# Scores in four quarters, zeros split around the attention, and weight pieces in fewer, larger transfers

## The chip, the cores and the metric

The kernel runs on one core of a Trainium2 chip. A core has a matrix engine (TensorE, "PE" in the profile, with its weight loads listed apart as "PEld"), a vector engine (DVE), a scalar engine (ACT), a general one (POOL), and a sync engine (SP) whose queue issues most DMAs. Sixteen DMA engines move the data between HBM and the on-chip memories. The metric is the device time of one execution in microseconds, the median of several runs.

## The reference

Two blocks follow each other. The first is attention in chunks: 4 batches x 8 heads, 768 positions of 64 numbers. Each chunk of 32 queries sees 8 memory keys, 16 positions to its left, itself, and 8 to its right. The second is a mixture of 8 experts over the 3072 resulting rows of 512 numbers: each row goes to the expert with the largest logit, each expert keeps at most 80 rows, and all other rows of the output are zero.

```python
scores = scale * np.matmul(q_c, k_full.transpose(0, 1, 3, 2))
a = np.exp(scores - max); a = a / sum(a)
out[:, :, c_start:c_end] = np.matmul(a, v_full)
...
x = attn_out.transpose(0, 2, 1, 3).reshape(B * S, H * D)
out = np.zeros((N, D))
for e in range(E):
    tok_idx = rows of expert e, the `capacity` with the largest gate weight
    h = np.maximum(x[tok_idx] @ w1[e], 0.0)
    out[tok_idx] = gate_w[tok_idx, None] * (h @ w2[e])
```

## The kernel before

**Attention** runs over 32 units (`units`, L770): a unit is one pair of heads and one half of the positions, so 384 queries per head. A unit's scores (`scores`, L773) are held transposed, keys on the 128 partitions and queries along the row: four groups of 96 queries, each with its own window of 128 keys (8 memory keys and 120 positions). First one bf16 matmul per head puts the mask into the whole score tile `sp` (L779), then four fp32 matmuls per head add keys times queries (L786). The two heads lie on partitions 0 to 63 and 64 to 127, so the two heads' matmuls use the two row halves of the array. The profile lists each fp32 matmul as two instructions. ACT then takes the exponential (L794), and the next iteration multiplies by the values (L357), in four column tiles of 32, and divides by the sum (L364, L366). Other work of a unit: transposes that put k and q into shape (L343, L315), transposes of the result for the gates (L375), and one step of the ranking that finds each expert's 80 best rows.

The order on each engine is written out by hand: `in_order` fixes the order in which the loop at L852 names the instructions. On the sync queue each iteration names, in this order, a load of k or q four units ahead (L889), the values six units ahead (L894), every fourth unit a store of finished rows into `xd` in HBM (L896), and then some bulk transfers (L897 to L905). Bulk means weights (`slow`) and zeros for the output (`nothing`).

**Weights.** Each expert has two matrices of 2 MB. Matrices are counted through, so matrix 2e is w1 of expert e and 2e+1 is w2 (`Weights`, L169). Nine have a place at once (WR = 9). Matrices 0, 1, 3 and 4 are loaded during the attention; matrix 2 lies where the k and q loads land (`ld`), so it is added to `slow` at unit NU - 6 = 26 (L897). Matrices 5 to 8 lie in memory that the attention gives up, and are loaded after it (L1143); 9 to 15 follow when an expert has freed a place (`load_next`, L1024). Each matrix is loaded in eight pieces of 256 KB: 128 rows of 512 numbers.

**Pacing.** From the end of the attention on, pieces go through `paced` (L162): each new piece waits until the one six before it has landed.

**Zeros** are 24 pieces of 128 output rows (L192), written from the tile `zero`. All of them fit into the loop.

**Experts** run in `run_experts` (L997), after an interlude in which the last ranks are found and the rows are gathered. For each expert: `up` (L1029, matmuls at L1043) with w1, `turn_in`, `store` of the one before, `down` (L1050, matmuls at L1057) with w2, and at the end `last` (L1065, matmuls at L1077). The scatter of an expert's rows into the output (L1111, L1099) comes after the zeros.

Of the kernel before, what the change touches and what calls it, by code (L numbers as in the profile page):

```python
# [12 lines left out]
F32 = mybir.dt.float32  # L13
# [11 lines left out]
NG = 4  # L25
# [37 lines left out]
def kernel(  # L63
# [13 lines left out]
    nc = tc.nc  # L77
    B, H, S, D = q.shape
    N, DM = out.shape
    E = moe_w_gate.shape[1]  # L80
    F = moe_w1.shape[2]
# [6 lines left out]
    NU = NR * HP  # L88
    DK = DM // 128
    FK = F // 128  # L90
# [3 lines left out]
    WR, WR0, WR2 = 9, 2, 2  # L94
# [9 lines left out]
    const = ctx.enter_context(tc.tile_pool(name="const", bufs=1))  # L104
# [24 lines left out]
    oneb = const.tile([128, 1], BF16, name="oneb")  # L129
    pref = const.tile([128, E], F32, name="pref")  # L130
    over_s = const.tile([128, NU, 2, NT], F32, name="over_s")
    zero = const.tile([128, DM], F32, name="zero")
    xg0 = const.tile([cap, DM], F32, name="xg0")
    xn0 = const.tile([128, HP, cap], F32, name="xn0")
    zerob = zero[:, :64].bitcast(BF16)
# [14 lines left out]
    follow = mybir.DependencyInfo(mybir.DependencyClass.Sync, mybir.DependencyReason.DATA)  # L150
# [8 lines left out]

    pieces = deque()  # L160

    def paced(dma):  # L162

        dma()
        pieces.append(list(nc.cur_bb.bb.instructions)[-1])
        if len(pieces) > 6:
            tc.add_manual_dep(pieces[-1], pieces.popleft().name, follow, reason="pieces")

    class Weights:  # L169
        def __init__(self, pools, tag):  # L170
# [2 lines left out]
        def load(self, i):  # L173
            src, nch = ((moe_w1, DK), (moe_w2, FK))[i % 2]
            s = i % len(self.pools)
            if i in self.given:
                t = self.given[i].rearrange("p a b -> p (a b)").rearrange("p (a b) -> p a b", a=nch)
            else:
                t = self.pools[s].tile(
                    [128, nch, DK * F // nch], F32, name=f"w{i}", tag=f"{self.tag}{s}", bufs=1  # L180
                )
            self.t[i] = t

            return [
                lambda c=c, f=f: nc.sync.dma_start(
                    t[:, c, f : f + 512], src[i // 2, c * 128 : c * 128 + 128, f : f + 512]
                )
                for c in range(nch)
                for f in range(0, DK * F // nch, 512)
            ]  # L190

    def zeros():  # L192
        zrows = 128
        return [
            lambda i=i: nc.sync.dma_start(
                out[i * zrows : (i + 1) * zrows, :].rearrange("(p r) d -> p r d", p=128),
                zero.unsqueeze(1),
            )
            for i in range(N // zrows)
        ]  # L200

# [506 lines left out]
    W = Weights([wpool] * (WR0 + 1 + WR2) + [None] * (WR - WR0 - 1 - WR2), "w")  # L708
    W.given[WR0] = wpool.tile([128, 4, F], F32, name="ld", tag=f"w{WR0}", bufs=1)

    with ExitStack() as actx:
# [61 lines left out]
        def scores(i):  # L773
            n, f = units[i]
            sp = [ps_s.tile([WK, NG, GQ], F32, name="sp", tag="s") for e in range(2)]

            for e in range(2):
                r = slice(64 * e, 64 * e + 64)
                nc.tensor.matmul(  # L779
                    sp[e].rearrange("p g q -> p (g q)"), lhsT=mkey[r, f, :], rhs=mqry[r, f, :],  # L780
                    start=True, stop=False,
                )
            for g in range(NG):
                for e in range(2):
                    r = slice(64 * e, 64 * e + 64)
                    nc.tensor.matmul(  # L786
                        sp[e][:, g], lhsT=at.kT[n][r, NG * f + g, :],
                        rhs=at.qT[n][r, HT * f + GQ * g : HT * f + GQ * g + GQ], start=False,
                        stop=g == NG - 1,
                    )  # L790
            P[i] = []
            for e in range(2):
                P[i].append(wk.tile([WK, NG, GQ], F32, name="P", tag="P"))
                nc.scalar.activation(P[i][e], sp[e], Act.Exp, scale=scale)  # L794
# [24 lines left out]
            turns[i] = turns.get(i, []) + [("k", n)]  # L819
            turns[i + 1] = turns.get(i + 1, []) + [("q", n)]  # L820

        later, done = deque(), deque()
        ranks = Ranks(gt, ps_x)
        start = len(list(nc.cur_bb.bb.instructions))
        def fill_in(n, cols=128):
# [26 lines left out]
        for i in range(NU):  # L852
            n, f = units[i]
            r = i // HP
            if i + 1 < NU:
                scores(i + 1)
            for kind, m in turns.get(i, []):
                if kind == "k":
                    at.turn_k(m)
                elif i >= 2:  # L860
                    at.turn_q(m)
            if i in constants:
                constants[i]()
            if i + 2 < NU:
                at.put_mv(*units[i + 2])
            if later:
                later.popleft()()
            if i:
                turn_x(i - 1)
            if i < 2:  # L870
                at.turn_q(i + 2)
            values(i)
            if i and i % HP == 0:
                lus[r] = ps_x.tile([128, 512], F32, name="lu", tag="t")
                steps = ranks.steps(r - 1, [xTs[i - HP + c] for c in range(HP)], lus[r])
                later = deque(
                    [lambda last=last, first=first: (last(), first()) for last, first in zip(later, steps)]
                    + steps[len(later) :]
                )
            if later:  # L880
                later.popleft()()
            if i == NU - 2:
                lp = at.pt[0]

                nc.tensor.matmul(lp[:, : NT * E], lhsT=zerob, rhs=zerob[:, : NT * E], start=True, stop=False)
                early([0, 1], lp)
            if i == NU - 1:
                early([2], lp)
            for kind, m in turns.get(i, []):  # L889
                (at.load_k if kind == "k" else at.load_q)(m + 2)  # L890
            if i % (2 * HP) == 1 and i + 7 < NU:
                at.load_mv(i // (2 * HP) + 1)
            if i + 6 < NU:
                at.load_v(*units[i + 6])  # L894
            if i and i % HP == 0:
                at.store(r - 1, xr[r - 1])  # L896
            if i == NU - 6:  # L897
                slow += W.load(WR0)
            for _ in range(2 if i >= 4 else 0):
                bulk = slow if slow and (i >= NU - 6 or i % 4 < 3) else nothing  # L900
                if bulk:
                    bulk.popleft()()
            for _ in range(2 if i >= 20 and i % 2 == 0 else 0):
                if nothing:
                    nothing.popleft()()  # L905
        turn_x(NU - 1)
        at.store(NR - 1, xr[NR - 1])
        assert not slow
        for dma in nothing:
            paced(dma)  # L910


        r = NR - 1
# [234 lines left out]
    with tc.If(redo[1] > 0):  # L1148

        with ExitStack() as actx:  # L1150
# [7 lines left out]
            at.load_mem(nc.sync)  # L1158
            at.clear()
            at.turn_mem(ps_t.tile([128, 512], F32, name="pm2", tag="t"))  # L1160
            for dma in zeros():
                dma()
            ranks = Ranks(gt, ps_t)
            for i, (n, f) in enumerate((HP * b + c, f) for b in range(B) for f in range(2) for c in range(HP)):
# [60 lines left out]
        with ExitStack() as fctx:  # L1225
            fw2 = fctx.enter_context(tc.tile_pool(name="fw2", bufs=1, reuse_waits="tile"))
            W2 = Weights([fw2] * 2, "v")
            for i in range(2):
                for dma in W2.load(i):
                    dma()  # L1230
            run_experts(fctx, "2", W2)

# [27 lines left out]
```

## Time and profile before

| what | value |
|---|---|
| median of 3 runs | 247.33 us (247.24 to 256.02) |
| span of the profiled execution | 246.5 us |
| TensorE busy | 228.3 us, 93% |
| weight loads busy | 200.6 us, 81% |
| DVE, ACT, POOL busy | 43%, 33%, 33% |
| moved by DMA | 70.97 MB, mean 288 GB/s |
| weight pieces | 128 of 256 KB, 5.2 us to land (the 8 of matrix 2: 6.0) |
| zeros | 24 pieces of 256 KB, 4.9 us to land |

The page's slices cut the span into 40 parts of 6.2 us; a digit is the busy share in tenths, and the last row is what the DMA engines moved.

```profile
PE   5979999999999999999899999969799997999980
PEld 3857889798888788888778889959799996999970
...
DMA  6999999999999999999999899999999998890101
GB/s 205 284 283 298 279 296 325 340 370 321 341 364 330 376 331 334 370 278 329 302 305 372 264 363 307 295 333 298 311 335 313 358 288 284 277 332 28 32 29 37
```

The attention fills the slices up to about the 22nd, the interlude the next two, the experts the rest. TensorE is nearly full in most slices, and so are the DMA engines until slice 36. A matmul's end is modelled, so a busy TensorE need not be one at its peak. Two of the groups that the change touches:

```profile
L786 PEld LDWEIGHTS sp<-qT,kT 64*128 64x128 f32 x512 | 33.2, 189 | 1.5 <-issue 0.9
L786 PE MATMUL sp<-qT,kT 64*128 64x96 f32 x512 | 33.5, 269 | 0.9 <-ACT qT L316 0.4
```

Here "64*128" says that 64 rows and 128 columns of the array hold weights; "64x96" is what streams through them.

### The profile page before, as it was taken

The numbers are of one execution on the slowest core, as the hardware profiler recorded it, in microseconds if no ns is written. First come the engines' busy times: TensorE is split into PE (matmuls) and PEld (weight loads), VectorE is DVE, ScalarE is ACT, GpSimd is POOL, SyncE is SP. The second block draws the span as 40 slices with busy tenths as digits, with TensorE's granted clock in tenths as the row PEclk, the third lists the DMA queues.
The fourth block names the chain that finished last, engine by engine and source line by source line (L and its number), as shares of the span: only waits on it lengthen the run. The fifth ranks groups of instructions, "written<-read, shape, count | busy, mean of one in ns | idle before, by whom it ended". The sixth has DMA issues, their size and how long they took to land. (4 is left out here: it accounts for less than half of the span.)

```text
span 246.5 us, 11417 instructions
## 1 busy us (share of the span) xinstructions
PE 228.3 (93%) x4976; PEld 200.6 (81%) x4976; DVE 105.5 (43%) x288; ACT 81.8 (33%) x198; POOL 80.5 (33%) x182
## 2 busy tenths in 40 slices
PE   5979999999999999999899999969799997999980
PEld 3857889798888788888778889959799996999970
DVE  3333447758579477585555862000112111110240
ACT  2245555665555573665545301100000101010000
POOL 2454947537275182450412147300101010110111
PEclk9999999999999999999999889989999999999996
DMA  6999999999999999999999899999999998890101
GB/s 205 284 283 298 279 296 325 340 370 321 341 364 330 376 331 334 370 278 329 302 305 372 264 363 307 295 333 298 311 335 313 358 288 284 277 332 28 32 29 37
DMA packets 69879, 70.97 MB, mean 288 GB/s; under 512 B 38204, under 2 KB 46396, under 8 KB 69820
## 3 DMA queue, kind: packets, MB, share of 16 engines
q1 hardware_dynamic: 67836, 67.17, 87.4%
q0 software_dynamic: 1024, 2.62, 3.5%
q8 instruction: 41, 0.67, 1.2%
q10 hardware_dynamic: 960, 0.36, 0.6%
q14 instruction: 18, 0.15, 0.2%
HBM read 56.24 MB, written 13.89 MB: 285 GB/s over the span
## 5 line engine op out<-in xcount | busy, mean ns | idle before, releaser
L794 ACT ACTIVATE P<-sp 128x384 f32<-128x384 f32 x64 | 27.9, 488 | 29.6 <-PE sp L786 29.6
L1043 PE MATMUL hp<-xn,w 128*64 128x80 f32 x896 | 33.7, 233 | 3.0 <-issue 3.0
L1043 PEld LDWEIGHTS hp<-xn,w 128*64 128x64 f32 x896 | 32.1, 137 | 3.9 <-issue 3.4
L786 PEld LDWEIGHTS sp<-qT,kT 64*128 64x128 f32 x512 | 33.2, 189 | 1.5 <-issue 0.9
L786 PE MATMUL sp<-qT,kT 64*128 64x96 f32 x512 | 33.5, 269 | 0.9 <-ACT qT L316 0.4
L1057 PE MATMUL yt<-hT,w 128*64 128x80 f32 x896 | 34.2, 239 | 0.0
L1057 PEld LDWEIGHTS yt<-hT,w 128*64 128x64 f32 x896 | 33.0, 142 | 1.2 <-issue 1.1
L1047 ACT ACTIVATE hT<-hp 128x320 f32<-128x320 f32 x16 | 7.0, 437 | 70.7 <-PE hp L1043 70.7
L1111 POOL DMA_INDIRECT out_dram<-y,idx_s x7 | 6.4, 917 | 73.0 <-DVE y L1110 73.0
L357 PE MATMUL o<-vw,P 128*32 128x65 f32 x1536 | 28.9, 222 | 0.7 <-issue 0.7
L357 PEld LDWEIGHTS o<-vw,P 128*32 128x32 f32 x1536 | 23.5, 109 | 6.3 <-issue 5.4
L346 DVE COPY kT<-pt 128x480 f32<-128x480 f32 x32 | 19.9, 666 | 16.3 <-PE pt L343 8.2
L268 POOL COPY vw<-mv 8x512 f32<-8x512 f32 x32 | 22.4, 703 | 8.7 <-DMA vw<-in_v_dram 8.7
L1022 DVE COPY xn<-xp 128x320 f32<-128x320 f32 x7 | 3.4, 491 | 39.4 <-PE xp L1020 39.4
L366 DVE TENSOR_TENSOR xr<-o,over_s 128x384 f32<-128x384 f32 x32 | 17.8, 558 | 1.1
L316 ACT COPY qT<-pt 128x384 f32<-128x384 f32 x31 | 16.0, 582 | 4.8 <-PE pt L315 4.8
L377 ACT COPY xT<-xt 128x384 f32<-128x384 f32 x32 | 15.7, 489 | 4.7 <-PE xt L375 4.7
L330 POOL COPY kh<-ld 128x768 f32<-128x768 f32 x15 | 12.3, 822 | 13.7 <-PE more L549 8.3
L375 PE MATMUL xt<-ident,xr 128*128 128x128 f32 x96 | 16.5, 281 | 0.0
L315 PE MATMUL pt<-ident,qh 128*128 128x128 f32 x96 | 15.0, 291 | 1.2 <-DVE kT L346 1.2
L1063 DVE COPY ys<-yt 128x320 f32<-128x320 f32 x7 | 3.4, 492 | 28.7 <-PE yt L1057 28.7
L531 DVE SCALAR_TENSOR_TENSOR less<-gbs,gw,behind 128x384 bf16<-128x384 f32 x21 | 15.0, 745 | 0.0
(162 smaller groups left out, 305.2 us busy)
## 6 DMA issues: line engine op xcount, KB each, us to landing
w<-in_moe_w_dram SPq DMA_DIRECT2D x120, 256.0 KB, 5.2
vw<-in_v_dram SPq DMA_DIRECT2D x60, 128.0 KB, 5.3
ld<-in_k_dram SPq DMA_DIRECT2D x16, 384.0 KB, 5.6
ld<-in_q_dram SPq DMA_DIRECT2D x16, 384.0 KB, 6.4
xd<-xr SPq DMA_DIRECT2D x8, 768.0 KB, 5.8
out_dram<-zero SPq DMA_DIRECT2D x24, 256.0 KB, 4.9
ld<-in_moe_w_dram SPq DMA_DIRECT2D x8, 256.0 KB, 6.0
vw<-in_v_dram SPq DMA_DIRECT2D x4, 96.0 KB, 5.6
```

The lines of the kernel that those rows point to most:

```text
L268: nc.gpsimd.tensor_copy(self.vw[n, f][:MS, :, :, :D], self.mv[b][:, h : h + 2].unsqueeze(2).to_broadcast([MS, 2, NG, D]),)
L315: nc.tensor.transpose(pt[:, t, :], qh[:, t0 + t].rearrange("p e d -> p (e d)"), ident)
L316: out[t0 // 3](qT.rearrange("p (x t) -> p x t", t=T0)[:, :, t0 : t0 + 3], pt.rearrange("p t x -> p x t"))
L346: nc.vector.tensor_copy(win[:, :, :, u0 : u0 + 3], _ap(pt, 0, [pt.ap[0], [JG, G], [1, (WK - MS) // T0], [step, 3]]),)
L357: nc.tensor.matmul(out[32 * i : 32 * i + 32, e, t, :], lhsT=P[e][:, g, CHUNK * c : CHUNK * c + CHUNK], rhs=self.vw[n, f][:, e, g, :], star ...
L366: nc.vector.tensor_tensor(out=xr[:, :, 128 * c : 128 * c + 128].rearrange("p t (e d) -> p e t d", e=2), in0=o[:, :, :, :D], in1=over_s[:, ...
L375: nc.tensor.transpose(xt[:, 128 * t : 128 * t + 128], xr[:, t, 128 * c : 128 * c + 128], ident)
L377: nc.scalar.copy(xT, xt[:, :HT])
L786: nc.tensor.matmul(sp[e][:, g], lhsT=at.kT[n][r, NG * f + g, :], rhs=at.qT[n][r, HT * f + GQ * g : HT * f + GQ * g + GQ], start=False, sto ...
L794: nc.scalar.activation(P[i][e], sp[e], Act.Exp, scale=scale)
L1043: nc.tensor.matmul(hp[j : j + 64, f, :], lhsT=w1[:, c, f1 : f1 + 64], rhs=xns[e][:, c, :], start=c == 0, stop=c == DK - 1,)
L1057: nc.tensor.matmul(yt[j : j + 64, d, :], lhsT=w2[:, f, d * 128 + j : d * 128 + j + 64], rhs=hTs[e][:, f, :], start=f == 0, stop=f == FK - 1,)
```

## The change

It has four parts.

- **Scores in quarters.** A window's 128 keys are loaded as two halves of 64 columns, so with the two heads there are four tiles of 64 x 64 in the array at a time, and twice as many matmuls. It is meant to load fewer columns per weight load. The mask's matmuls stay as they were.
- **Fewer, larger packets.** w1 is loaded in four pieces of 512 KB with rows of 4 KB; w2 keeps eight of 256 KB. Zeros go out in 12 pieces of 512 KB, for which the tile `zero` becomes twice as wide (its second memset grows from 256 to 768 columns). A piece now carries its size in units of 256 KB, and `paced` keeps at most six units in flight.
- **Bulk from the second unit, by a budget.** From i = 1 on, each unit adds 2 to `due`, and pieces go out while it is above zero; one in six is a piece of zeros. Before, weights began at i = 4.
- **Half of the zeros behind the attention.** Six of the 12 pieces are held back in the loop and go out paced, ahead of matrix 5.

In the changed text the condition that adds matrix 2 to `slow` at unit NU - 6 stands twice, so its pieces are queued twice, to the same place.

```diff
-    zero = const.tile([128, DM], F32, name="zero")
+    zero = const.tile([128, 2 * DM], F32, name="zero")
...
-    def paced(dma):
-
+    def paced(piece):
+
+        size, dma = piece
         dma()
-        pieces.append(list(nc.cur_bb.bb.instructions)[-1])
-        if len(pieces) > 6:
-            tc.add_manual_dep(pieces[-1], pieces.popleft().name, follow, reason="pieces")
+        ins = list(nc.cur_bb.bb.instructions)[-1]
+        last = None
+        while sum(n for n, _ in pieces) + size > 6:
+            last = pieces.popleft()[1]
+        if last is not None:
+            tc.add_manual_dep(ins, last.name, follow, reason="pieces")
+        pieces.append((size, ins))
...
             return [
-                lambda c=c, f=f: nc.sync.dma_start(
-                    t[:, c, f : f + 512], src[i // 2, c * 128 : c * 128 + 128, f : f + 512]
-                )
+                (FK // nch, lambda c=c: nc.sync.dma_start(
+                    t[:, c, :], src[i // 2, c * 128 : c * 128 + 128, :]
+                ))
                 for c in range(nch)
-                for f in range(0, DK * F // nch, 512)
             ]
 
     def zeros():
-        zrows = 128
+        zrows = 256
         return [
-            lambda i=i: nc.sync.dma_start(
-                out[i * zrows : (i + 1) * zrows, :].rearrange("(p r) d -> p r d", p=128),
-                zero.unsqueeze(1),
-            )
+            (2, lambda i=i: nc.sync.dma_start(
+                out[i * zrows : (i + 1) * zrows, :].rearrange("(p r) d -> p (r d)", p=128), zero
+            ))
             for i in range(N // zrows)
         ]
...
-            for e in range(2):
-                r = slice(64 * e, 64 * e + 64)
+
+            quarters = [(e, slice(64 * e, 64 * e + 64), slice(h, h + 64)) for e in range(2) for h in (0, 64)]
+            for e, r, _ in quarters[::2]:
                 nc.tensor.matmul(
                     sp[e].rearrange("p g q -> p (g q)"), lhsT=mkey[r, f, :], rhs=mqry[r, f, :],
                     start=True, stop=False,
                 )
             for g in range(NG):
-                for e in range(2):
-                    r = slice(64 * e, 64 * e + 64)
+                for e, r, h in quarters:
                     nc.tensor.matmul(
-                        sp[e][:, g], lhsT=at.kT[n][r, NG * f + g, :],
+                        sp[e][h, g], lhsT=at.kT[n][r, NG * f + g, h],
                         rhs=at.qT[n][r, HT * f + GQ * g : HT * f + GQ * g + GQ], start=False,
...
-        later, done = deque(), deque()
+        later, due, moved = deque(), 0.0, 0
...
             if i == NU - 6:
                 slow += W.load(WR0)
-            for _ in range(2 if i >= 4 else 0):
-                bulk = slow if slow and (i >= NU - 6 or i % 4 < 3) else nothing
-                if bulk:
-                    bulk.popleft()()
-            for _ in range(2 if i >= 20 and i % 2 == 0 else 0):
-                if nothing:
-                    nothing.popleft()()
+            if i == NU - 6:
+                slow += W.load(WR0)
+            if i >= 1:
+                due += 2.0
+            while due > 0 and (slow or len(nothing) > 6):
+
+                turn = slow if slow and (moved % 6 < 5 or len(nothing) <= 6) else nothing
+                size, dma = turn.popleft()
+                dma()
+                due -= size
+                moved += 1
...
-        for dma in nothing:
-            paced(dma)
+        for piece in nothing:
+            paced(piece)
```

More of the change, by code (lines that the diff above doesn't have):

```diff
@@ L1160 @@
             at.turn_mem(ps_t.tile([128, 512], F32, name="pm2", tag="t"))
-            for dma in zeros():
+            for _, dma in zeros():
                 dma()
@@ L1228 @@
             for i in range(2):
-                for dma in W2.load(i):
+                for _, dma in W2.load(i):
                     dma()
```

## The prediction

> **What bounds the kernel now.** I read the table of windows first, since the kernel has two stages with different habits: attention (to about 138 us) and experts (from 151 us). Its columns are PE, PEld, DVE, ACT and POOL busy, then granted clock, DMA share and GB/s.
>
> ```profile
> 60.00:80.00 20.00, 20.00 (x442) 16.84 (x444) 15.21 (x42) 11.07 (x27) 10.03 (x21) 1.00 1.12 343
> 120.00:140.00 20.00, 19.27 (x428) 16.23 (x424) 13.52 (x41) 9.03 (x23) 2.41 (x9) 1.00 0.93 318
> 160.00:170.00 10.00, 7.72 (x160) 7.38 (x156) 0.60 (x2) 0.44 (x1) 0.00 (x0) 0.83 0.98 321
> 190.00:200.00 10.00, 10.00 (x264) 9.56 (x262) 1.68 (x3) 0.87 (x2) 0.91 (x1) 1.00 0.96 329
> 220.00:230.00 10.00, 10.00 (x280) 9.72 (x277) 1.24 (x2) 0.87 (x2) 1.22 (x2) 1.00 0.21 69
> ```
>
> TensorE and the DMA engines are both full to 220 us, so busy shares can't tell which one sets the end. The waits can. TensorE's waits between 18 and 140 us have no DMA in them worth naming, and over the whole span the only long ones of the experts are "issue", for which the profile shows no releaser (engine and line, what it waited for: us in all, times, longest):
>
> ```profile
> PE pt L315 <- DVE kT L346: 0.8, 2, 0.6
> PE o L357 <- issue: 0.7, 1, 0.7
> PE sp L786 <- issue: 0.2, 1, 0.2
> ```
>
> ```profile
> PE hp L1043 <- issue: 5.3, 3, 2.3
> ```
>
> So TensorE sets the pace of both stages and the DMA keeps just ahead. How far ahead is the number that matters here. The chain that ended last doesn't tell it: it breaks off at 235 us, at a scatter. The timeline does, first TensorE's last matrices (start, length, line; L1043 is a first matrix, L1057 and L1077 a second), then the issues on the sync queue:
>
> ```profile
> 206.59 1.47 PE L1043 MATMUL hp<-xn,w 128*64 128x80 f32 x36 [1.74 <-issue]
> ...
> 213.33 4.87 PE L1043 MATMUL hp<-xn,w 128*64 128x80 f32 x128
> ...
> 223.47 4.60 PE L1043 MATMUL hp<-xn,w 128*64 128x80 f32 x128
> ...
> 228.56 4.65 PE L1057 MATMUL yt<-hT,w 128*64 128x80 f32 x128
> 233.04 0.72 PE L1077 MATMUL yt<-hT,w 128*64 128x80 f32 x16
> ```
>
> ```profile
> 210.81 0.33 SPq L185 DMA_DIRECT2D w<-in_moe_w_dram  x1
> ```
>
> ```profile
> 137.64 0.38 SPq L381 DMA_DIRECT2D xd<-xr  x1
> 138.13 14.15 SPq L185 DMA_DIRECT2D w<-in_moe_w_dram  x17
> ```
>
> The piece issued at 210.81 is the last of the last expert's first matrix (tile 14, counting matrices from 0); the view of DMAs says that it took 6.3 us to land:
>
> ```profile
> w<-in_moe_w_dram SPq DMA_DIRECT2D x1, 256.0 KB, 6.3
> ```
>
> So tile 14 is there at 217.1 and is first used at 223.4: 6.3 us of slack. In the same way tile 12 has 12.5 us (200.9 against 213.3), and tile 15 9.6 us (223.4 against 233.0). The 88 paced pieces from 138.13 to 218.44 go out back to back, 0.91 us each: the slack shrinks with every expert, because TensorE needs about 10 us an expert and the DMA 14.7 us.
>
> **What the skill says.** "TensorEngine Tiling (Array Packing)", Key Properties: tiles work in parallel, but a change of the tiling mode drains the array. The trace agrees on both. L357's four 32-column tiles start 7 ns apart and repeat every 57 ns; after them a 64x128 matmul starts 151 ns after the last one instead of about 55, and from 128x128 transposes to 128x64 matmuls (L1108 to L1057) it is 202 ns where 109 is usual: some 95 ns. "TensorE: Matmul & The Clock Gate", LDWEIGHTS: a weight load takes columns/1.2 ns, 107 for 128 and 53 for 64. In the trace the scores' pairs repeat every 111 ns, and after a switch to 64 columns the second pair comes 53 ns late. "Runtime: NRT & Kernel Launch", Instruction fetch mechanics: 16 KiB blocks of 256 instructions, fetched by a DMA queue. The page's q8 has 41 such packets; one of 2.1 us began at 203.1, just ahead of TensorE's gap at 204.6.
>
> **Scores in quarters (L779, L786).** Before, per unit, from single records: the mask takes 170 ns, the eight score pairs 84 + 6 x 111 = 753 ns from first to last, and the next transpose starts 202 ns later: 1125 ns. The pairs are bound by the 128-column load (111), not by the stream: experts' pairs with 80 columns repeat every 69 ns, that is 80 x 2/2.4 + 2.5, so 96 columns would take 82.5. After: 16 instructions become 32 in eight groups of four. If the mask (64x128) to the quarters (64x64) counts as a switch, which no run shows: 160 + 95 to the first group, 53 + 83 to the second, six times 83, then 80 + 95 to the next: 1064 ns. Saved: 61 ns x 32 = 2.0 us. If it doesn't: 170 + 7 x 83 + 175 = 926 ns, 6.4 us. I take 2.0, as every other change of columns in this trace pays. The 1,024 further instructions are 4 more fetch blocks; attention then needs one every 4.7 us, near the experts' 4.4.
>
> **What moves in the attention loop.** Count in units of 256 KB. Before: 40 of weights and 24 of zeros, 64 from unit 4 on. After: 32 for four matrices, 12 of zeros, and tile 2 twice, because the line that adds W.load(WR0) at NU - 6 now stands twice: 16. That is 60, from unit 1 on. TensorE doesn't wait for DMA there, so a lighter loop gains nothing; the earlier start loads DMA engines that are full already (share 1.1 to 1.2 from 10 to 30 us), but k and q are loaded four units, 16 us, ahead, and v six. Both cost 0. With `due` saved up over three empty units, tile 2's first copy goes out at once at NU - 6, and the second waits for it on the sync queue; behind it stand only xd stores. Cost 0, hidden by units 27 to 31. The memset at L724 grows from 256 columns (0.27 us) to 768 (0.8 us); VectorE idles 2.1 us after it for k's first load. Cost 0.
>
> **Zeros behind the attention.** Six pieces of 512 KB are paced ahead of tile 5: 12 units in the queue before the weights, and tile 2's double keeps the loop from having taken them. The start moves up by 2.0 us, 2.5 units at the 0.80 us of 138 to 151. So the weights are 9.5 units late; at 0.95 us a unit (71 pieces from 151.0 to 218.44) that is 9.0 us. Larger packets: 1536 bytes take 65 ns and 2048 take 84 (medians), so about 8 ns a packet is fixed. 2560 packets fewer in five first matrices and 768 in the zeros, over 16 engines, give back 1.7 us. Against it: three pieces of 512 KB in flight instead of six of 256 leave on average 5 units in flight and not 5.5, 9% less; if latency sets the rate, the five first matrices (40 units) lose 3.4 us, if the engines do, nothing. I let these cancel: 9.0, between 7.3 and 12.
>
> **The sum.** Tile 14 lands at 217.1 + 9.0 = 226.1; TensorE would be there at 223.4 - 2.0 = 221.4 and stands for 4.7 us. From tile 14 on nothing changes, so the end moves by 226.1 - 223.4 = +2.7 us. Tile 15 lands about 232.4 and is wanted at 235.7; tile 12 at 209.9, wanted at 211.3: no wait. After its 2.3 us gap at 160.5 TensorE was throttled and one matrix took 6.06 us instead of 4.42; I count half of that 1.6 us, 0.8. 247.3 + 2.7 + 0.8 = 250.8 us.
>
> **Rivals.** (A) No drain: 6.4 us saved, the start 8 units earlier, the weights 4 units or 3.8 us late, less 1.7 for packets: tile 14 at 219.2 against a need of 217.0, so the end moves by -4.2: 243.1 us, and under 242.4 if a fetch stall goes too. For it: the weights of the quarters could load under the mask's 160 ns, as they do now. Against: 95 ns at every other change of columns. (B) The queue is latency bound in the large pieces, or the fetches stall attention: 12 us late, the full 1.6 for the clock: 217.1 + 12 - 223.4 + 1.6 = +7.3, 254.6 us, slower. For it: pieces need 5.2 us to land, and 6 x 256 KB in 5.2 us is just the 300 GB/s seen. Against: the DMA share is 0.95. (C) The zeros are hidden: the delay stays within the slack (under 4.3 us), TensorE still sets the end, 247.3 - 2.0 = 245.3. Against: twelve units are 9 us at any rate seen in this stage.
>
> **Chances.** Forecast 0.42, A 0.13, B 0.27, C 0.18. Slower by over 2% (above 252.3): most of B (0.23) and a fifth of the forecast (0.09), 0.32. Faster (below 242.4): half of A, a little of C, and 0.04 for what I don't see: 0.13. The range from 244 to 255.5 leaves out half of A and the upper third of B.
>
> **What would show it.** Right: score groups of four every 83 ns, and a gap of about 255 ns from mask to scores; zeros issued from about 135.6 us and tile 5 some 9 us after; a wait of TensorE at L1043 ended by a DMA of w before the last expert, with no such wait now. Wrong: no wait of TensorE for w (then C or A), score groups slower than 100 ns, or waits for w at earlier experts (B).

## The result: 273.5 us, ten per cent slower

The changed kernel takes 273.47 us (median of 4 runs, 271.08 to 277.21) beside 247.55 us for the kernel before; the ratio is 1.102, 95% interval 1.093 to 1.111. Forecast were 250.8 us, with a range to 255.5. Some executions of any version run a few per cent longer at a lower granted clock; medians include them and ratios don't, so where a version had too few others no ratio is given.

The span grew from 246.5 to 271.4 us, in two places. The first matmul of an expert comes at 168.6 us instead of 150.9 (+17.7), and from there to the last matmul it takes 96.0 us instead of 88.8 (+7.2).

First the profile's table of windows (PE, PEld, DVE, ACT and POOL busy, granted clock, DMA share, GB/s), at the stretches shown of before, and one more:

```profile
60.00:80.00 20.00, 19.14 (x503) 14.97 (x503) 13.14 (x40) 10.55 (x29) 9.12 (x23) 1.00 0.97 300
120.00:140.00 20.00, 18.19 (x504) 13.91 (x497) 12.62 (x36) 10.85 (x27) 5.79 (x15) 1.00 0.63 200
160.00:170.00 10.00, 7.53 (x109) 6.79 (x110) 4.55 (x23) 0.42 (x1) 5.62 (x10) 0.93 0.97 329
190.00:200.00 10.00, 9.82 (x253) 9.27 (x251) 1.87 (x5) 0.87 (x2) 0.95 (x1) 1.00 0.91 303
220.00:230.00 10.00, 9.29 (x248) 8.84 (x242) 1.68 (x3) 0.87 (x2) 0.91 (x1) 1.00 0.95 322
230.00:240.00 10.00, 6.68 (x130) 6.27 (x129) 0.00 (x0) 0.81 (x2) 0.00 (x0) 0.83 0.89 311
```

In these two stretches of the attention TensorE was idle for 0 and 0.7 us before; now it is for 0.9 and 1.8 us. In the first of them it issues 503 matmuls instead of 442. At 230 us it stands still for a third of the time, while the DMA engines are busy. The waits name both losses (engine and line, what it waited for: us in all, times, longest):

```profile
PE hp L1049 <- DMA w<-in_moe_w_dram: 6.7, 6, 2.4
PE o L359 <- issue: 6.2, 7, 1.8
PE sp L788 <- issue: 5.6, 4, 2.6
PE hp L1049 <- issue: 4.0, 4, 2.5
...
PE pt L317 <- issue: 1.4, 1, 1.4
```

"issue" means that nothing in the profile released the engine. In the attention it was about 1 us before and is some 13 us now, on whatever line stands there. The timeline of TensorE shows what such a wait looks like, and the waits for w (start, length, line, then the idle time before and its releaser):

```profile
28.86 0.89 PE L788 MATMUL sp<-qT,kT 64*64 64x96 f32 x32
...
31.89 0.71 PE L788 MATMUL sp<-qT,kT 64*64 64x96 f32 x19
34.51 0.55 PE L788 MATMUL sp<-qT,kT 64*64 64x96 f32 x13 [1.90 <-issue]
...
99.08 0.88 PE L788 MATMUL sp<-qT,kT 64*64 64x96 f32 x31
102.56 0.29 PE L788 MATMUL sp<-qT,kT 64*64 64x96 f32 x1 [2.60 <-issue]
...
229.85 0.36 PE L1049 MATMUL hp<-xn,w 128*64 128x80 f32 x4 [0.71 <-DMA w<-in_moe_w_dram]
232.61 0.36 PE L1049 MATMUL hp<-xn,w 128*64 128x80 f32 x4 [2.40 <-DMA w<-in_moe_w_dram]
233.89 5.69 PE L1049 MATMUL hp<-xn,w 128*64 128x80 f32 x116 [0.92 <-DMA w<-in_moe_w_dram]
...
248.20 4.23 PE L1049 MATMUL hp<-xn,w 128*64 128x80 f32 x116 [2.17 <-DMA w<-in_moe_w_dram]
```

A unit's 32 score matmuls should run through in 0.89 us. At 32.4 us they stop after 19, at 99.7 after 31: no data and no buffer can be missing in the middle of one group that reads one tile.

**What stands at those points.** I numbered TensorE's instructions (weight loads, matmuls and the semaphore waits between them) in order of time. The eleven longest gaps of the attention come at numbers 705, 961, 1473, 1729, 1985, 2241, 3777, 4033, 5569, 6081 and 6337: each is 193 more than a multiple of 256. The instruction queue q8 moves packets of 16 KB, one for every 256 instructions; the profile lists 45 of them, before it was 41:

```profile
q8 instruction: 45, 0.74, 1.1%
```

Worked out from the single records, for some of these boundaries (us; "wait" is from passing the boundary before to the start of the packet, "use" is how long TensorE took over the 256 instructions, "gap" is from the start of the last instruction ahead of the boundary to that of the first behind it):

```
kernel   number  use   packet starts  wait  packet took  landed to passed  gap
before     961   5.12      30.91      1.06     1.09           2.98         0
before    4801   5.31     119.88      3.32     1.47           1.46         0.95
before    6337   4.49     160.19      4.35     1.10           1.55         2.51
after      961   4.13      32.02      3.79     1.10           1.39         2.15
after     1985   4.73      56.54      4.13     0.95           1.36         1.71
after     4033   4.16      99.97      4.41     1.09           1.49         2.84
after     9921  10.58     229.46      2.22     0.96           7.40         0
after    10689   5.00     250.37      0.03     1.18           3.79         0
```

A packet is sent for when the boundary before has been passed, takes about 1.0 us, and its instructions can run some 1.3 us after it has landed (1.2 to 1.6 wherever there is a gap). Where the DMA engines are idle, after 250 us, the wait ahead of it is nearly nothing; where they are full it is mostly 2 to 4 us. TensorE stands when wait + 2.3 us is more than the use. In the attention of before the mean wait was 2.3 us and a block lasted 5.6; in the changed kernel it is 2.8, and a block lasts 4.9 without the gaps (4.4 where a gap follows). The shorter block counts for more than the longer wait: the profiled executions of all versions with before's attention and pieces have mean waits of 2.2 to 2.7 us. Less the usual step of some 0.1 us each, the gaps at boundaries sum to 15.8 us in the attention (13 of over 0.3 us), before to 1.3 us (2 of them). In the experts it is the other way round, 1.2 us against 5.9.

Clock was lost besides. The page's slices (6.8 us each) show 0.7 of full speed in the sixth and the sixteenth, right after stops of 2.2 and 2.8 us, and again in the 35th, where TensorE waits for w. They show the thin DMA of the emptied loop, too:

```profile
PE   5989698979999968999798996899999998596980
...
PEclk9999979999999997999999999899999999799997
DMA  7999999998999996987937199999999999893101
```

The sync queue shows the zeros in front of the weights (start, length, line):

```profile
154.28 0.38 SPq L383 DMA_DIRECT2D xd<-xr  x1
154.70 9.07 SPq L198 DMA_DIRECT2D out_dram<-zero  x6
165.22 4.75 SPq L189 DMA_DIRECT2D w<-in_moe_w_dram  x7
```

### The profile page after: what moved, and what is told of

It is laid out like the page before. It is cut to its first block, busy times and chain, and to the rows that moved or that the text cites. A ratio compares the mean times of both kernels' runs of the same rounds, so it can differ in the third digit from the quotient of the medians.

```text
span 271.4 us, 12413 instructions
## 1 busy us (share of the span) xinstructions
PE 234.5 (86%) x5488; PEld 196.9 (73%) x5488; DVE 105.0 (39%) x288; ACT 82.3 (30%) x198; POOL 79.1 (29%) x182
## 3 DMA queue, kind: packets, MB, share of 16 engines
q0 software_dynamic: 1024, 2.62, 3.1%
## 5 line engine op out<-in xcount | busy, mean ns | idle before, releaser
L1049 PE MATMUL hp<-xn,w 128*64 128x80 f32 x896 | 38.2, 245 | 10.7 <-DMA w<-in_moe_w_dram 6.7
L1049 PEld LDWEIGHTS hp<-xn,w 128*64 128x64 f32 x896 | 35.7, 147 | 12.4 <-DMA w<-in_moe_w_dram 7.6
L359 PE MATMUL o<-vw,P 128*32 128x65 f32 x1536 | 31.7, 228 | 6.2 <-issue 6.2
L788 PE MATMUL sp<-qT,kT 64*64 64x96 f32 x1024 | 30.0, 250 | 6.0 <-issue 5.6
L359 PEld LDWEIGHTS o<-vw,P 128*32 128x32 f32 x1536 | 25.1, 113 | 13.0 <-issue 12.7
L1063 PEld LDWEIGHTS yt<-hT,w 128*64 128x64 f32 x896 | 32.0, 137 | 1.8 <-issue 1.6
L788 PEld LDWEIGHTS sp<-qT,kT 64*64 64x64 f32 x1024 | 23.3, 133 | 12.7 <-issue 12.0
L270 POOL COPY vw<-mv 8x512 f32<-8x512 f32 x32 | 20.9, 656 | 1.7 <-DMA vw<-in_v_dram 1.6
L332 POOL COPY kh<-ld 128x768 f32<-128x768 f32 x15 | 12.3, 823 | 18.7 <-issue 10.9
L457 POOL TENSOR_TENSOR desc<-oh,masks 128x24 bf16<-128x24 bf16 x16 | 3.3, 227 | 46.9 <-DVE over_s L366 36.3
L366 DVE RECIPROCAL over_s<-o 128x6 f32<-128x6 f32 x32 | 6.2, 194 | 23.5 <-PE o L359 23.4
```

Source lines behind the costliest of these rows:

```text
L270: nc.gpsimd.tensor_copy(self.vw[n, f][:MS, :, :, :D], self.mv[b][:, h : h + 2].unsqueeze(2).to_broadcast([MS, 2, NG, D]),)
L359: nc.tensor.matmul(out[32 * i : 32 * i + 32, e, t, :], lhsT=P[e][:, g, CHUNK * c : CHUNK * c + CHUNK], rhs=self.vw[n, f][:, e, g, :], star ...
L788: nc.tensor.matmul(sp[e][h, g], lhsT=at.kT[n][r, NG * f + g, h], rhs=at.qT[n][r, HT * f + GQ * g : HT * f + GQ * g + GQ], start=False, sto ...
L1049: nc.tensor.matmul(hp[j : j + 64, f, :], lhsT=w1[:, c, f1 : f1 + 64], rhs=xns[e][:, c, :], start=c == 0, stop=c == DK - 1,)
L1063: nc.tensor.matmul(yt[j : j + 64, d, :], lhsT=w2[:, f, d * 128 + j : d * 128 + j + 64], rhs=hTs[e][:, f, :], start=f == 0, stop=f == FK - 1,)
```

## The experiments

Three theories. **Blocks**: the quarters shorten TensorE's instructions but double their number, and blocks of instructions then come too late behind a full DMA. **Zeros**: what is held back behind the attention delays the weights. **Packets**: the larger pieces are slower. In what follows, "gaps" are the summed gaps at block boundaries in the attention, from the profiled execution of each version.

### The quarters alone, and all but the quarters

```diff
# q_only: the kernel before, with this part of the change alone
-                        sp[e][:, g], lhsT=at.kT[n][r, NG * f + g, :],
+                        sp[e][h, g], lhsT=at.kT[n][r, NG * f + g, h],
# no_q: the changed kernel, with this part undone
```

> The kernel before with the scores in quarters and nothing else changed. Theory F (TensorE's instruction blocks are used up faster than they are fetched: 32 more instructions a unit, a block of 256 lasts some 4.5 us, a fetch takes 2.4 us plus its wait in the DMA queues): at least 8 us of TensorE gaps in attention, all at the same place modulo 256 instructions, and 255 to 264 us in all. Rival T (the traffic of the change makes the gaps: bulk from unit 1, packets of 4 KB, tile 2 loaded twice): no such gaps, 2 us gained, 244 to 247 us.

Measured: 263.31 us, ratio 1.056 (1.036 to 1.077). Gaps 12.2 us, first expert matmul at 165.6 us.

> The changed kernel with the scores of the kernel before, all else as changed. Theory F: attention ends (last xd store) within 3 us of the kernel before's 137.6; the weights then are 12 units late instead of 9.5, so TensorE waits some 5 us for tile 14 and the end is at 251 to 256 us. Rival T: the gaps in attention stay, attention ends at 148 or later, 262 to 272 us.

Measured: 262.18 us, ratio 1.055 (1.040 to 1.069). Gaps 5.0 us, first expert matmul at 158.9; first matrix behind the attention 10.9 us after the last xd store, instead of 0.5; TensorE waits 3.9 us for w. The last xd store comes at 143.2 us, 5.5 later than before, which neither expectation had. So the loss has two halves of similar size, and each stands without the other.

### The quarters without traffic

```diff
# q_quiet: q_only, and all bulk of the loop behind it
-            for _ in range(2 if i >= 4 else 0):
...
-        for dma in nothing:
+        for dma in list(slow) + list(nothing):
             paced(dma)
```

> The kernel before with quarters, and every weight and zero piece of the loop moved behind the loop (paced); the total is longer for that, only attention is read. If a fetch waits behind bulk transfers in the DMA queues, it now starts within 1 us of a block's end, there are under 2 us of gaps, and the last xd store is issued at about 135.6 us, 2.0 before the kernel before's 137.6: the gain of the quarters by themselves. If the gaps don't depend on the traffic, they stay, and the store comes after 143 us.

Measured once: 298.13 us, since all weights come late. What counts is the attention. The windows of q_quiet, then of q_only:

```profile
60.00:80.00 20.00, 20.00 (x555) 15.73 (x544) 14.59 (x38) 12.23 (x31) 11.90 (x24) 1.00 0.77 208
80.00:100.00 20.00, 20.00 (x522) 15.67 (x525) 15.26 (x41) 11.09 (x27) 9.76 (x21) 1.00 0.85 240
```

```profile
60.00:80.00 20.00, 18.66 (x477) 14.64 (x470) 12.52 (x32) 11.09 (x27) 10.72 (x24) 1.00 1.12 341
80.00:100.00 20.00, 18.82 (x477) 14.57 (x465) 13.12 (x36) 11.54 (x28) 8.98 (x21) 1.00 1.09 332
```

The same instructions run without a gap at a DMA share of 0.77 to 0.85, and with 1.2 to 1.3 us of gaps in 20 us at 1.1. The mean wait of a block is 1.6 us instead of 2.7; all 4.3 us of gaps (under 2 were expected) lie before 57 us, where q_quiet too has a share of 0.83 to 1.14. The last xd store comes at 139.8 us; less the gaps that is 135.5, near the 135.6 expected. Units without a gap take 3.52, 3.87 and 4.38 us here and 3.56, 3.91 and 4.43 before: the quarters themselves gain some 45 ns a unit.

### More instructions without the quarters

```diff
# pad32: the kernel before; of the 24 value matmuls per unit, 8 are done twice
+                for i in range(4 if t == 0 else 0):
+                    nc.tensor.matmul(out[32 * i : 32 * i + 32, e, t, :], ... same operands ...)
```

> The kernel before with 8 of a unit's 24 value matmuls done twice: 32 instructions more a unit as in the quarters, 57 ns for each four matmuls, 7.3 us in all, and no new tiling. Theory F: the gaps of the quarters appear here too, at least 4 us in attention on top of the 7.3, so 258 us or more. Rival M (the quarters' own tiling makes the gaps): 7.3 us longer and no more gaps than before, 254 to 255 us.

Measured once: 263.95 us. A block lasts 5.25 us instead of 5.63, gaps 4.5 us instead of 1.3. The last xd store comes 6.8 us late, but the interlude takes another 8 us more: a block came 1.55 us late at 138 us, and the clock afterwards was low.

```profile
137.00:150.00 13.00, 11.67 (x183) 10.43 (x182) 6.34 (x19) 3.41 (x9) 0.44 (x2) 0.72 0.38 121
150.00:165.00 15.00, 13.27 (x115) 11.36 (x115) 6.83 (x29) 0.99 (x5) 6.33 (x13) 0.67 1.02 346
```

Gaps grew by 3.2 us where at least 4 were expected; in the quarters, whose blocks are shorter still (4.9 us), they are far larger. That denser instructions make gaps fits this, but one execution doesn't show it: versions below with no instruction more have gaps of 4.1 to 5.0 us. The time as such can't be put down to them either: the added matmuls cost TensorE work too.

### The double load, the zeros, the packets

```diff
# no_q_no_dup: no_q, matrix 2 queued once
             if i == NU - 6:
                 slow += W.load(WR0)
-            if i == NU - 6:
-                slow += W.load(WR0)
# no_q_no_both: that, and all zeros in the loop, with room in the budget for them
-                due += 2.0
+                due += 2.2
-            while due > 0 and (slow or len(nothing) > 6):
+            while due > 0 and (slow or nothing):
...
-                turn = slow if slow and (moved % 6 < 5 or len(nothing) <= 6) else nothing
+                turn = slow if slow and (moved % 3 < 2 or not nothing) else nothing
# big_only: the kernel before with its own schedule, but the larger pieces
```

> The changed kernel with the scores of before, and tile 2 queued once. It measured 262.2 us with the double. Theory F2 (every byte ahead of the weights of the experts delays them at 0.95 us a unit, wherever it stands): 8 units less, but in a loop that has room for them, so the first paced weight piece goes out no more than 3 us earlier than 154.1, and 257 to 262 us. Rival D (the double load is what makes the experts late): 7 us earlier, 253 to 256 us.

Measured: 261.52 us, ratio 1.042 (1.025 to 1.059): the double load is worth little, and less than the intervals of this and of no_q can tell.

> The same with all zeros in the loop as well (budget 2.2 units so that they fit). Left of the change: larger packets and bulk from unit 1. Theory F2 (the zeros held back are what makes the experts late): the first paced weight piece within 1.5 us of the last xd store, no TensorE wait for w, and what is left over 247 us is gaps in attention: 248 to 253 us. Rival L (large packets slow the paced queue): TensorE still waits for w, 254 us or more.

Measured: 251.63 us (20 runs), ratio 1.005 (1.001 to 1.009). The zeros' place, with the budget that goes with it, is worth the 9.9 us between these two. In the traces, whose spans are 11.8 us apart, 3.8 us come before the first expert matmul, where gaps fell from 4.7 to 0.6 us, and 8.2 us in the experts (98.4 against 90.1 us); the first weights follow the last xd store after 0.5 us instead of 10.9. TensorE's waits in no_q_no_dup:

```profile
PE hp L1048 <- issue: 5.8, 6, 2.5
PE hp L1048 <- DMA w<-in_moe_w_dram: 5.1, 4, 2.3
```

With the zeros in the loop there is no wait for w at all.

> The kernel before with the larger packets alone: first matrices in 4 pieces of 512 KB, zeros in 12, order and times of issue as before, three of the large pieces in flight. Theory P (a fetch waits for a packet ahead of it, so packets twice as long make it wait longer): mean wait of a fetch in attention 0.4 us over before's 2.3, 3 to 6 us of gaps in attention, 250 to 256 us. Rival S (the size of packets doesn't matter; early bulk does): wait 2.1 to 2.5 us, 245 to 249 us.

Measured: 252.96 us, ratio 1.015 (1.002 to 1.028). The paced pieces take 81.4 us from first to last issue instead of 80.3: large pieces are neither faster nor slower there. In the attention the mean wait is 2.6 us and the gaps are 4.1, near theory P's figures. But no_q_no_both, with the same pieces, has the same mean wait and gaps of only 0.6, so the size of the pieces isn't shown to be the cause.

### The quarters in the rest of the change

```diff
# q_no_both: the changed kernel with matrix 2 queued once and all zeros in the loop
# (the budget and the turns as in no_q_no_both)
-            while due > 0 and (slow or len(nothing) > 6):
+            while due > 0 and (slow or nothing):
```

> The changed kernel with tile 2 loaded once and all zeros written inside the attention loop again (quarters, larger packets and the earlier start of the bulk stay). Fetch theory: the quarters' loss doesn't need the other parts; TensorE's gaps at every 256th instruction stay at 10 to 15 us in the attention, the last xd store is issued near 150 to 153 us, the first paced weight follows it at once, and no wait of TensorE for w over 3 us is left: 262 to 265 us. Rival (the zeros and the double load are what fills the DMA queues, so the stalls are theirs): attention ends within 3 us of before, 250 to 253 us.

Measured: 263.9 us, ratio 1.073 (1.062 to 1.084), gaps 15.8 us, just those of the changed kernel, the last xd store at 151.5 us. The block theory's number; but waits of 4.6 us for w remain where none over 3 were expected, with the zeros out of the way. That left a question open.

```profile
PE o L359 <- issue: 5.7, 7, 1.5
PE sp L788 <- issue: 4.9, 5, 1.5
PE hp L1047 <- DMA w<-in_moe_w_dram: 4.6, 4, 1.9
```

### Fewer transfers under way

```diff
# q_loop3: q_only, bulk of the loop held to three pieces in flight
-                    bulk.popleft()()
+                    paced(bulk.popleft(), 3)
# pace4, pace5, pace8: the kernel before with 4, 5 or 8 instead of 6
-        if len(pieces) > 6:
+        if len(pieces) > 4:
```

> The kernel before with the quarters, and with the bulk pieces inside the attention loop held to three in flight (each waits for the landing of the third before it; before, nothing in the loop waited). Fetch theory: a shallower queue lets an instruction block start sooner; its mean wait falls from 2.7 us to 2.2 or less, the gaps at 256 instructions from 12.2 us to under 4, the last xd store moves from 151 to 140 to 144 us, 250 to 255 us in all. Rival 1 (the loads of k, q and v make the wait, not the bulk): gaps of 10 us and more remain, 261 us or more. Rival 2 (the sync queue now stands behind its own waits): k, q and v come late, and TensorE waits for copies of them for 5 us or more.

Measured: 262.91 us, ratio 1.069 (1.058 to 1.080). Half a hit: the mean wait of a block falls from 2.7 to 2.3 us and the gaps from 12.2 to 8.8, not under 4; the first expert matmul comes 7.1 us earlier than in q_only, at 158.5. But the sync queue is behind, the last xd store goes out at 153.0 us, and TensorE then stands 5.0 us for gathered rows. The wait fell by no more than it differs between executions of before's attention (2.2 to 2.7 us), so how much of it the bulk in flight makes this run doesn't settle.

> The kernel before with at most 4 pieces in flight behind the attention instead of 6. If a fetch waits behind what is in flight, the mean wait in the experts' stage falls from 1.9 to about 1.3 us and the three gaps of 2.5, 1.5 and 2.0 us go; the weights come later (4 x 256 KB in flight): if their 6.3 us of slack hold, 241 to 245 us. If the rate falls with the pieces in flight (two thirds of 300 GB/s), TensorE waits for w: 255 us or more.

Measured: 264.25 us, ratio 1.061 (1.048 to 1.075). No gap over 0.3 us at a block boundary in the experts any more, where before had 5.9 us, and 10.4 us of waits for w in their place:

```profile
PE hp L1043 <- DMA w<-in_moe_w_dram: 10.4, 7, 2.6
```

> The kernel before with eight pieces of 256 KB in flight behind the attention instead of six. Fetch theory: the DMA engines are busy 96% of that stage already, so the rate hardly rises, but an instruction block waits behind more descriptors: mean wait of the experts from 1.9 us to 2.5, gaps at 256 instructions from 5.9 us to 7 to 9, 248 to 251 us. Rival (latency sets the rate, as four in flight suggests): the last paced piece is issued 10 us or more earlier, and the time stays at 247 or falls a little, since TensorE doesn't wait for weights.

Measured: 254.02 us (249.67 to 257.84) beside 247.73 of before. Gaps of the experts 7.6 us, mean wait there 2.1 us and not 2.5. The rival was right on the rate: the last piece is issued at 206.4 us, 12 us earlier. It doesn't pay.

> The kernel before with five pieces in flight behind the attention. Fetch theory: the wait of a block falls below 1.9 us and the gaps of the experts from 5.9 us to 0 to 3; the weights come some 4 to 6 us later at the end, which the slack of 6.3 us at tile 14 takes: 244 to 249 us, possibly better than before. Rival: the rate falls as it did with four in flight (265 GB/s instead of 325), halfway; tile 14 is 8 us late and TensorE waits for w: 251 to 255 us.

Measured: 254.86 us, ratio 1.028 (1.013 to 1.042). The rival's case: gaps of the experts fall to 2.7 us, but TensorE waits 4.3 us for w, though the slack that I had read should have covered it.

### The order in which the matrices are queued

Two experiments now showed waits for w where a slack of 6.3 us was supposed to be. Reading `run_experts` again: `up(e + 1)` stands ahead of `down(e)`, and each queues one matrix. So the order on the queue is 9, 11, 10, 13, 12, 15, 14, and the last eight pieces are not those of matrix 15 but of matrix 14. The packets say so too: in the changed kernel those of 4 KB belong to first matrices, and the last 2 MB of them are moved between 239.5 and 247.6 us, when those of 2 KB have ended (240.0).

```diff
# after_order, nqnd_order (of no_q_no_dup), before_order, pace5_order (of pace5)
-            load_next(2 * e + len(W.pools))
+            if e == 0:
+                load_next(len(W.pools))
...
             load_next(2 * e + 1 + len(W.pools))
+            load_next(2 * e + 2 + len(W.pools))
```

> The changed kernel with the matrices 9 to 15 loaded in the order of their numbers. As written they are queued 9, 11, 10, 13, 12, 15, 14, because up(e + 1) stands ahead of down(e) and each queues one, so 14 comes last of all and is wanted before 13 and 15. Queue theory (what the late zeros cost the experts is the wait for 12 and 14, which have no slack in this order): both land some 7 us sooner, TensorE's waits for w fall from 6.7 us to under 2, first expert matmul to last matmul from 96.0 us to 89 to 92, and the time from 273.5 to 266 to 270 us. Rival (the experts are slow for the throttled clock, or the rate of the DMA as such): 272 us or more, waits for w stay over 4 us.

Measured: 270.36 us, ratio 1.085 (1.062 to 1.109), but against other runs of before than the change's. In the trace the waits for w are gone, and the experts take 87.8 us instead of 96.0, a larger gain than expected:

```profile
PE hp L1049 <- issue: 4.5, 6, 2.4
PE o L359 <- issue: 0.9, 1, 0.9
PE yt L1064 <- issue: 0.6, 1, 0.6
```

The whole gains less than 8 us, since this execution lost 4.3 us in the interlude, at a clock of 0.51 to 0.61.

> The same order of loading in the changed kernel without quarters and with matrix 2 loaded once (the zeros are still held back). Queue theory: first expert matmul to last matmul from 98.4 us to 90 to 93, as where the zeros lie in the loop (90.1), and 261.5 us become 253 to 257. Rival: 260 us or more.

Measured: 255.86 us, ratio 1.024 (1.000 to 1.048), where no_q_no_dup had 1.042; waits for w 5.1 to 0 us, experts 98.4 to 92.5, the upper end of what was expected.

> The same order of loading in the kernel before, where matrix 14 lands at 223.4 us and is first used at 223.5. Queue theory: it lands at 216 to 217, TensorE didn't wait for it, so the time stays within 1% of 247.5. Rival (the order costs already): 244 us or less.

Measured: 256.79 us (248.98 to 257.63) beside 252.34 (248.06 to 255.67): no verdict on the time, beyond that the order alone isn't seen to help. The last piece of matrix 14 is issued at 211.8 us instead of 218.4; when it landed, the trace doesn't show.

> The kernel before with the same order of loading and five pieces in flight instead of six. With five alone TensorE waited 4.3 us for w. Queue theory: the order gives some 7 us of slack, so those waits go (under 1 us), and fewer instruction blocks come late than with six: 245 to 249 us, perhaps the best of all. Rival: the waits were not for 12 and 14, and 252 us or more remain.

Measured: 251.0 us (246.38 to 256.61) beside 252.34 of before. Waits for w 4.3 to 0 us, gaps of the experts 0.7 us. The mechanism came as expected, so the same kernel was timed more often:

> The kernel before with matrices 9 to 15 queued in the order of their numbers and five pieces in flight, timed in more rounds, because it is the one version that may beat both kernels. If the order has bought the slack that a slower and shallower queue needs, and fewer instruction blocks come late in the experts, it is 0.5 to 1.5% faster than before (ratio 0.985 to 0.995). Rival: the two runs of 246.4 and 247.2 us were the better end of the spread, and the ratio is 1.00 within its interval.

Measured: 247.92 us (22 runs) beside 249.0, ratio 0.999 (0.992 to 1.006). The rival: no version was found that beats the kernel before.

## Why the prediction was wrong

**Scores in quarters: right in size.** The forecast was a drain of 95 ns at the mask, groups every 83 ns, and 61 ns saved a unit. Measured: 263 ns from mask to first group (255 predicted), 173 ns from the last to what follows (175), 0.65 us from first to last (0.63), and some 45 ns a unit, 1.4 us in all instead of 2.0.

**"The 1,024 further instructions are 4 more fetch blocks": the step that failed first.** The four blocks are there (45 packets), and "one every 4.7 us" was good (4.9 without the gaps). What I made of it was wrong: I counted them as nothing because the experts live with 4.4 us. The experts don't: their three gaps, 5.9 us, were in the profile as "issue", and I had named one of them a late packet. The skill's "Runtime: NRT & Kernel Launch", Instruction fetch mechanics, says that the next page is fetched while the current one runs and that crossing a boundary is mostly hidden; in these traces it is hidden only where a block lasts longer than the wait + 2.3 us, which is 4.6 us on the mean in before and 5.1 after. The term measured 14.5 us instead of 0. Rival B had fetches that stall the attention, but as one of two ways to a total of 7.3 us.

**"A lighter loop gains nothing": wrong too.** With the quarters in, traffic in the attention delays not TensorE's data but its instructions: q_quiet against q_only has gaps of 4.3 us instead of 12.2.

**The zeros: right in delay, wrong in slack.** Six pieces took 10.5 us ahead of matrix 5, at 0.88 us a unit (0.80 predicted, 9.6 us). The shift of 2.5 units for an earlier end of the attention didn't come, since the attention ended later. But "tile 14 is there at 217.1 ... 6.3 us of slack" was the reading of the wrong matrix. I took the queue to hold the matrices in order of number. It is matrix 15 that is there at 217.1; the piece issued at 218.44 lands at 223.4 and is the last of matrix 14, which TensorE first uses at 223.5. Its landing in the kernel before, by the view of DMAs (us to landing at the end):

```profile
w<-in_moe_w_dram SPq DMA_DIRECT2D x1, 256.0 KB, 5.0
```

There is no slack, and every us of delay reaches the end. With that one correction the working gives 247.3 + 9.0 + 0.8 = 257.1 us, and with the 14.5 us of gaps on top 271.6. That this is near the 273.5 measured is in part luck: it leaves out what the next paragraphs list. In no_q_no_dup against no_q_no_both the experts lost 8.2 us. The experts of after_order give 8.2 us back, of which only 6.7 are waits; the rest fits the clock, since in the changed kernel the matrix that followed three waits took 5.69 us for 116 matmuls, the last one 4.23.

**Packets, double load, memset, early start: nothing found against it.** The memset and the early start weren't tested apart. Large pieces in flight didn't lose 9%, nor gain 1.7 us that could be seen: 81.4 against 80.3 us, though big_only as a whole is 1.5% slower (0.2 to 2.8%). The first mask is at 10.9 us, at 10.8 before.

**The sum as it came out.** Attention to the last xd store, 16.6 us: 14.5 more of gaps, 1.4 less for the quarters; the other 3.5 fit the low clock, 0.83 in two stretches of 10 us. The execution of q_no_both speaks for it: it has the same gaps and no low clock in the attention, and its last xd store comes at 151.5 us, 2.8 earlier. Interlude 1.0. Experts 7.2: 6.7 of waits for w and 3.5 in the first expert's first matrix, with 4.7 us fewer gaps at boundaries on the other side; the remaining 1.7 us weren't traced further.

The 1.0 and the 3.5 can't be put down to the change. TensorE writes the first expert's rows, ACT copies them, and only then can the matrices start. In before ACT's copy started 0.04 us after TensorE's last matmul for it, in the changed kernel 2.5 us after. The interlude grew by only 1.0 us, since in before a part of it ran at a low clock (0.83 from 140 to 150 us). The two copies (before, then after; "remote" is a releaser that the profile doesn't name further):

```profile
150.44 0.43 ACT L992 COPY xn<-pt 128x320 f32<-128x320 f32 x1 [6.20 <-PE pt L988]
```

```profile
168.11 0.42 ACT L998 COPY xn<-pt 128x320 f32<-128x320 f32 x1 [8.74 <-remote]
```

The first matrix then took 8.6 us to the start of the second, in before 5.1. Of the 19 profiled executions 13 have a late copy (2.1 to 2.5 us) and then 8.3 us or more for that matrix; the other 6 have 0.04 us. The kernel of pace5_order, profiled twice, shows both. So some 4.5 of the 24.9 us between the two profiled spans come from something that varies between executions of one kernel.

**What stays open.** Seven executions with the attention of before (before, pace4, pace5, pace8 and the three with another order) have gaps of 0.2 to 2.8 us there. no_q, no_q_no_dup, nqnd_order and big_only, without quarters but with larger pieces, have 4.1 to 5.0, while no_q_no_both, with larger pieces too, has 0.6. Whether it is the size of pieces or when they fall within a unit isn't settled, nor what makes ACT's copy late.

## What to carry to other kernels

Count instructions as well as time: where an engine's instructions are fetched through busy DMA engines, splitting an instruction in two can cost more in late instruction blocks than it saves, and unexplained idle time ("issue") at regular instruction numbers is the sign of it in the profile before. Slack of a transfer is worked out from the order in which the program queues it and the order in which it is used, which are both to be read from the code, never from the numbers of the tiles. And a change that costs nothing by itself may take the slack that another needs: here the zeros used slack that wasn't there.

## What the runs showed of the hardware

- The waits of instruction blocks follow the load: about 0.1 us with idle DMA engines, 1.6 us on the mean in q_quiet, 2.3 in before (2.2 to 2.7 in other executions of its attention), 2.8 in the changed kernel; then 1.0 us for the packet and 1.3 us to use.
- A DMA share of 0.96 in the experts wasn't the limit. From first to last issue the 88 paced pieces took 95.6 us with four in flight, 85.3 with five, 80.3 with six, 67.6 with eight. The rate rises with the bytes in flight: with the first matrices in pieces of 512 KB and the same bytes in flight they took 81.4 us.
- The same interlude took 13.3 us in before, 18.6 in after_order and 21.0 in pad32, the last two with windows at a granted clock of 0.51 to 0.72. In pad32 a stop of 1.55 us comes just before; that a stop brings the low clock on wasn't tested.
